# A new table of due times for a planned attention and expert kernel, and two products of zeros ahead of early scores

## The chip, the cores and the metric

One core of one Trainium2 chip runs the whole program. The metric is the device time of one execution in microseconds (us), the median of several runs. The trace comes from one execution taken by the hardware profiler.

## The reference

The inputs are q, k and v of 8 batches, 8 heads, 576 positions and 64 elements, gate weights, and two weight matrices. The first half is attention in a window: each position looks at itself and at the 63 positions ahead of it.

```python
scores = scale * np.matmul(q, k.transpose(0, 1, 3, 2))
mask = (rel >= 0) & (rel < 64)
scores = np.where(mask, scores, -1000000000.0)
attn = softmax(scores)              # max subtracted, + 1e-09 in the sum
x = (attn @ v) as (8, 576, 512)
```

The second half scores each of a batch's 576 rows of x against the gate weights, picks the 128 highest, and adds to these rows alone a gated two-layer product:

```python
top_idx = np.argpartition(-scores[b], 128)[:128]
xe = x[b, top_idx]
out[b, top_idx] = xe + sigmoid(scores[b, top_idx])[:, None] * (np.maximum(xe @ w1, 0) @ w2)
```

w1 is 512 x 1024, w2 is 1024 x 512, all in float32.

## The kernel before

**Attention.** The 8 x 9 blocks of 64 positions are taken two at a time, as 36 pairs m (`attend`). For a pair, SP loads q, k and v. PE computes the scores in 32 products (`go_s`, L533) into PSUM room s0, the only one of its kind. For pairs 0 to 8, DVE adds the mask and takes the maxima (L554), ACT the exponentials (L563), PE transposes (L571) and ACT copies (L579). From pair 9 on (`fold`), ACT and DVE merge the two key blocks that a row sees (L594, `copy_predicated` L599), DVE takes the maximum (L606), and after the transposes DVE and GpSimd part them again (L639, L645). PE multiplies by v into PSUM room av, also the only one (`go_pv`, L714). ACT takes out the sums (L734), DVE inverts them (L738) and scales (L742). Then DVE forms the gate score of the 128 rows, the **gate dot** (`gate_dot`, L517), with two inputs from SBUF, and SP stores the rows.

**Choice and experts.** When a batch's five pairs have their gate scores (pair 4 closes batch 0), `choose` ranks the rows with comparisons on DVE (L843, L854) and counts on PE (L898, L939). GpSimd then gathers the chosen rows from DRAM (L963). `moe` transposes them (L988) and forms the two expert products on PE (L1055 or L1120, and L1167) for the groups of batches (0), (1), (2), (3), (4, 5), (6, 7). Each float32 product is made of three, from a high and a low part of both sides. The weights are loaded in 16 steps of 256 KB, eight of w1 and eight of w2, and GpSimd splits each into its parts: **hi** (L484) and **lo** (L488).

**The order.** Every operation is entered with `add` into a list of 1919, with an engine, a planned duration and a due time. `Order.run` plans the whole program before it is issued: at each step it looks, for each engine, at the operations whose predecessors and rooms are planned, finds the earliest start t0, and takes the one with the smallest due among those that can start within SLACK of t0. An operation with a late due is still taken if nothing else can start. DVE operations marked `port` (gate dots, comparisons) with a due under BEFORE may be taken if they can start within YIELD of t0. The order so found is the order of the instructions on each engine, and there is no other choice on the chip; each engine waits in that order for its semaphores. PLACE shifts the due time of single operations, named by their number in the list: loads are 5 to 116, weight steps from 118 on in threes (load, hi, lo), and attention begins at 166. Number 232 is the scores of pair 2 and 265 the scores of pair 3. The same planner carries constants for what it believes of the chip: LINK (a delay between engines ahead of PE), TURN (a change of PE's tile mode), RATE (bytes per us of the transfers), PHASE, FETCH and FRESH (PE's instruction fetch).

After the scores of pairs 0, 1 and 2 the kernel already issues a product of zeros into another PSUM room (`keep_warm`, L310): 256, 256 and 128 columns.

Of the kernel before, what the change touches and what calls it, by code (L numbers as in the profile page):

```python
# [21 lines left out]
P = 128  # L22
# [5 lines left out]
STEP = 4.61  # L28
EASE = 1.1
BEGIN = 6.8  # L30
LINK = {"PE": 0.3404}
TURN = 0.25
RATE = 350700.0
FLIGHT = 6
FIRST = 10
PLACE = {
# [24 lines left out]
}  # L61
PREV = 0.5
CUR = 0.2
BEFORE = 37.46
YIELD = 1.885
FETCH = 256
PHASE = 193
FRESH = 3.401
KEEP = {0: 2, 1: 2, 2: 1}
WARM = 8  # L70
DIRECT = (0,)
# [19 lines left out]
class Order:  # L91
# [3 lines left out]
    def __init__(self):  # L95
        self.ops = []
        self.room = {}
        self.where = {}
        self.tiles = {}

    def rooms(self, kind, names):
        for n in names:
# [4 lines left out]
    def add(self, *a, **kw):  # L107
        op = Op(*a, **kw)
        op.due += PLACE.get(len(self.ops), 0.0)
        self.ops.append(op)  # L110
        return op

# [14 lines left out]
    def run(self, engines, free):  # L127
        for op in self.ops:
            op.left = len(op.after)
            for a, _ in op.after:  # L130
                a.then.append(op)
        held = {"DVE": (0.0, 0.0), "POOL": (0.0, 0.0)}
        avail = {e: [] for e in engines}
        for op in self.ops:
            if not op.left:
                avail[op.eng].append(op)
        mode = None
        wire = 2.0
        flight = []
        code = WARM * 4  # L140
        marks = {}

        def fetched(op, t):
            end = code + op.code
            k = (end - PHASE) // FETCH
            need = PHASE + FETCH * k
            if need <= code or need - FETCH not in marks:
                return t
            share = (need - code) / op.code
            return max(t, marks[need - FETCH] + FRESH - share * op.pitch)  # L150
        done = 0
        self.log = []
        while done < len(self.ops):
            best = None
            for e in engines:
                cand = []
                for op in avail[e]:
                    t, picks = self.ready(op)
                    if t == float("inf"):
                        continue  # L160
                    t = max(t, free[e])
                    if op.port:
                        a, z = held["POOL" if e == "DVE" else "DVE"]
                        if a <= t < z:
                            t = z
                    if op.code:
                        t = fetched(op, t)
                    if op.size and e == "SP" and len(flight) >= FIRST:
                        t = max(t, flight[-FLIGHT] + 0.1)
                    cand.append((t, op.due, op, picks))  # L170
                if not cand:
                    continue
                t0 = min(c[0] for c in cand)
                same = e == "PE" and mode == 64
                c = min((c for c in cand if c[0] <= t0 + SLACK.get(e, 0.0)
                         or c[2].port and c[2].due < BEFORE and e == "DVE" and c[0] <= t0 + YIELD
                         or same and c[2].mode == mode and c[0] <= t0 + STAY),
                        key=lambda c: (same and c[2].mode != mode, c[1]))
                if best is None or c[0] < best[0]:
                    best = c  # L180
            assert best is not None, [(e, [o.due for o in avail[e]]) for e in engines]
            t, _, op, picks = best
            if op.mode and mode and op.mode != mode:
                t = max(t, free["PE"] + TURN)
            for (key, kind), n in zip([k for k in op.take if k[0] not in self.where], picks):
                self.where[key] = n
                self.room[n] = float("inf")
            op.start = t
            if op.code:
                for need in range(PHASE - FETCH, 1 << 20, FETCH):  # L190
                    if need >= code + op.code:
                        break
                    if need >= code:
                        marks[need] = t + (need - code) / op.code * op.pitch
                code += op.code
            if op.mode:
                mode = op.mode
            if op.port:
                held[op.eng] = (t, t + op.pitch)
            free[op.eng] = t + op.pitch  # L200
            if op.size:
                begin = max(wire, t + op.pitch + 0.25)
                wire = begin + op.size / RATE
                op.end = max(wire, begin + 0.2) + 1.997
                if op.eng == "SP":
                    flight.append(op.end)
            else:
                op.end = t + op.dur
            for key in op.give:
                self.room[self.where[key]] = op.end + 0.1  # L210
            avail[op.eng].remove(op)
            for o in op.then:
                o.left -= 1
                if not o.left:
                    avail[o.eng].append(o)
            self.log.append((t, op))
            op.go()
            done += 1


STAY = 0.2035
SLACK = {"PE": 0.00835, "DVE": 0.02651, "ACT": 0.06129}


@with_exitstack
def tile_attention_moe(ctx: ExitStack, tc, q, k, v, wg, w1, w2, outs, B, H, S, D, C):
    nc = tc.nc
# [10 lines left out]
    order = Order()  # L238
# [47 lines left out]
    def make(key, shape, dtype, space="sb", sub=""):  # L286
        tag = order.where[key] + sub
        serial[0] += 1
        t = (p_ps if space == "ps" else p_sb).tile(
            shape, dtype, tag=tag, name=f"{key[0]}{sub}{'_'.join(map(str, key[1:]))}")  # L290
        order.tiles[key, sub] = t
        return t

    def get(key, sub=""):
        return order.tiles[key, sub]

    warm = const.tile([P, P], F32, name="warm")
# [913 lines left out]
    free = {"PE": 2.0, "ACT": 2.6, "DVE": 2.0, "POOL": 6.2, "SP": 0.8}  # L1211
# [40 lines left out]
```

## Time and profile before

| | |
|---|---|
| median of 3 runs | 248.06 us (247.59 to 249.39) |
| the profiled execution | 246.34 us |
| its span, first to last instruction | 244.6 us |
| mean granted clock of TensorE | 0.979 |
| PE busy | 222.1 us (91%) |
| DVE busy | 188.1 us (77%) |
| ACT busy | 149.3 us (61%) |
| POOL busy | 120.1 us (49%) |
| moved by DMA | 47.22 MB |

PE is TensorE's products (PEld its weight loads), DVE is VectorE, ACT is ScalarE, POOL is GpSimd, SP issues transfers. Busy times are sums over the whole span and hide that the stages differ, so the rows below go by stage. The granted clock is that of TensorE as a share of 2.4 GHz; a stretch with 0.5 runs at 1.2 GHz.

### The profile page before, as it was taken

How to read it: one execution, taken by the hardware profiler on the slowest of the kernel's cores; microseconds unless marked ns; L12 is line 12 of the kernel's file. 1: busy time of each engine (PE TensorE's matmuls, PEld its weight loads, DVE VectorE, ACT ScalarE, POOL GpSimd, SP SyncE). 2: the span in 40 equal slices, each digit the busy share in tenths (PEclk: the TensorE clock that was granted, in tenths of full speed). 3: DMA queues.
4: the chain of work that ended last, by engine and by line, in shares of the span. 5: the costliest groups of instructions: out<-in, count | busy, mean ns of one | idle time of the engine just before them, and what ended most of it. 6: DMA issues, size and time to landing. Idle time of an engine off the chain costs nothing. (4 is left out here: it accounts for less than half of the span.)

```text
span 244.6 us, 10376 instructions
## 1 busy us (share of the span) xinstructions
PE 222.1 (91%) x4298; PEld 186.7 (76%) x4298; DVE 188.1 (77%) x560; ACT 149.3 (61%) x478; POOL 120.1 (49%) x160
## 2 busy tenths in 40 slices
PE   8679695949999999999899999989999999999991
PEld 7567584837877778787678888868878898899891
DVE  0587879797898989999997799999997996352220
ACT  2798865445998798797459977847896231022000
POOL 7885867892042535286048725762752581130031
PEclk9999989797999999999999999999999999999999
DMA  6998999896656698687558657354443221120011
GB/s 212 369 338 280 342 335 337 271 335 217 217 159 223 235 321 291 213 240 265 212 178 295 218 157 225 96 196 146 124 143 89 88 90 43 43 82 6 0 46 43
DMA packets 25167, 47.22 MB, mean 193 GB/s; under 512 B 2976, under 2 KB 4000, under 8 KB 25120
## 3 DMA queue, kind: packets, MB, share of 16 engines
q1 hardware_dynamic: 23680, 42.10, 52.3%
q0 software_dynamic: 1296, 4.20, 5.0%
q8 instruction: 34, 0.56, 0.9%
q10 hardware_dynamic: 144, 0.26, 0.3%
q14 instruction: 13, 0.11, 0.1%
HBM read 35.01 MB, written 11.53 MB: 190 GB/s over the span
## 5 line engine op out<-in xcount | busy, mean ns | idle before, releaser
L616 ACT ACTIVATE p<-p,nm 128x64 f32<-128x64 f32 x216 | 59.2, 341 | 0.4
L645 POOL TENSOR_TENSOR pt<-pt,past 128x512 f32<-128x512 f32 x27 | 35.8, 1328 | 41.7 <-ACT pt L630 35.9
L533 PE MATMUL s<-k,q 64*64 64x128 f32 x1152 | 43.0, 287 | 8.4 <-DVE p L599 3.3
L714 PEld LDWEIGHTS av<-v,pt 64*64 64x64 f32 x2176 | 40.0, 138 | 10.7 <-issue 7.9
L714 PE MATMUL av<-v,pt 64*64 64x65 f32 x2176 | 44.1, 226 | 3.3 <-issue 2.7
L533 PEld LDWEIGHTS s<-k,q 64*64 64x64 f32 x1152 | 34.2, 141 | 16.2 <-issue 5.1
L517 DVE CUSTOM_DVE_ANT_0 jk<-x,wgb 128x512 bf16<-128x512 f32 x36 | 34.0, 945 | 0.2
L563 ACT ACTIVATE p<-p,nm 128x128 f32<-128x128 f32 x72 | 23.7, 394 | 12.5 <-DVE nm L554 12.5
L1167 PE MATMUL yp<-w2l,hh 128*128 128x512 f32 (+1 forms) x72 | 27.4, 381 | 0.0
L1167 PE MATMUL yp<-w2h,hl 128*128 128x512 f32 (+1 forms) x72 | 27.4, 381 | 0.0
L1167 PE MATMUL yp<-w2h,hh 128*128 128x512 f32 (+1 forms) x72 | 27.4, 383 | 0.0
L742 DVE TENSOR_TENSOR x<-av,z 128x512 f32<-128x512 f32 x36 | 24.6, 684 | 1.1
L554 DVE CUSTOM_DVE_ANT_0 p<-s,mask 128x128 f32<-128x128 f32 x72 | 16.2, 285 | 11.2 <-PE s L533 11.1
L599 DVE COPY_PREDICATED p<-live,s 128x512 f32<-128x512 uint8 x27 | 19.7, 731 | 3.1 <-ACT p L594 3.1
L624 PE MATMUL t<-ident,p 128*128 128x128 f32 x108 | 20.8, 282 | 0.0
L594 ACT COPY p<-s 128x512 f32<-128x512 f32 (+1 forms) x27 | 15.8, 585 | 6.7 <-PE s L533 4.3
L1199 POOL DMA_INDIRECT out_dram<-xe,idx x7 | 7.4, 1052 | 25.2 <-DVE xe L1190 22.0
L924 POOL TENSOR_SCALAR sel<-slots,diff 128x128 bf16<-128x128 f32 x20 | 16.3, 822 | 6.5 <-DVE diff L908 3.2
L639 DVE TENSOR_TENSOR pt<-t,own 128x512 f32<-128x512 f32 x27 | 18.2, 675 | 1.7 <-PE t L624 1.6
L630 ACT COPY pt<-t 128x512 f32<-128x512 f32 x27 | 15.7, 583 | 4.9 <-DVE pt L639 3.4
L1120 PE MATMUL hp<-xgh,w1l 128*128 128x256 f32 x64 | 18.1, 284 | 0.0
L606 DVE TENSOR_REDUCE nm<-p 128x8 f32<-128x512 f32 x27 | 17.9, 664 | 0.1
(115 smaller groups left out, 462.3 us busy)
## 6 DMA issues: line engine op xcount, KB each, us to landing
v<-in_v SPq DMA_DIRECT2D x36, 260.0 KB, 3.9
q<-in_q SPq DMA_DIRECT2D x36, 256.0 KB, 3.9
out_dram<-x SPq DMA_DIRECT2D x32, 256.0 KB, 3.8
k<-in_k SPq DMA_DIRECT2D x31, 256.0 KB, 4.6
st<-in_w SPq DMA_DIRECT2D x16, 256.0 KB, 4.8
k<-in_k SPq DMA_DIRECT2D x8, 128.0 KB, 4.7
out_dram<-x SPq DMA_DIRECT2D x8, 128.0 KB, 3.3
k<-in_k ACTq DMA_DIRECT2D x1, 256.0 KB
```

The lines of the kernel that those rows point to most:

```text
L517: nc.vector.tensor_tensor_reduce(out=junk()[:n, :E], in0=xf[:n], in1=wgb[:n], op0=ALU.mult, op1=ALU.add, scale=1.0, scalar=0.0, accum_out=acc)
L533: nc.tensor.matmul(s[c * W:(c + 1) * W, r, j], get(("q", m))[rs, j, c], keys(m, c, j, rs), start=True, stop=True)
L563: nc.scalar.activation(pe[:, j, :, r], pe[:, j, :, r], AF.Exp, bias=st_nm[m][:, r, j:j + 1], scale=-1.0)
L599: nc.vector.copy_predicated(out=get(("p", m)).rearrange("p j r w -> p r j w"), mask=live.unsqueeze(1).unsqueeze(1).to_broadcast([P, 2, NP, ...
L616: nc.scalar.activation(pe[:, j, r], pe[:, j, r], AF.Exp, bias=st_nm[m][:, 1, j, r:r + 1], scale=SCALE)
L624: nc.tensor.transpose(get(("t", m, 0))[:, j, :], get(("p", m))[:, j].rearrange("p r w -> p (r w)"), ident)
L639: nc.vector.tensor_tensor(out=parts(make(("pt", m, 1), [P, NP, P], F32)), in0=parts(get(("t", m, 0))), in1=spread(own), op=ALU.mult)
L645: nc.gpsimd.tensor_tensor(out=pt, in0=pt, in1=spread(past), op=ALU.mult)
L714: nc.tensor.matmul(av[cs, r, j * D1:(j + 1) * D1], pt[a][rs, j, cs], get(("v", g // 2))[rs, g % 2, j], start=a == 0 or o == c, stop=a == 1)
L742: nc.vector.tensor_tensor(out=x.rearrange("p j r d -> p r j d"), in0=avv()[:, :, :, :D], in1=st_z[m][:, 1].unsqueeze(3).to_broadcast([P, 2 ...
L1120: nc.tensor.matmul(get(hk)[:, j], w[:, c, js], get(xk, a)[:, c].rearrange("p u c -> p (u c)"), start=(n == 0), stop=(n == 3 * KC1 - 1))
L1167: nc.tensor.matmul(get(yk)[:C, :e1 - e0], get((a, gi, c // per))[:, c % per, u * C:(u + 1) * C], w[:, c, e0:e1], start=(n == 0), stop=(n = ...
```

## The change

The table PLACE gets 195 entries in place of 168, with three decimals; 78 operations stand in both. The planner's constants LINK, TURN, RATE, BEFORE, YIELD, FRESH, STAY and SLACK get new values. For the scores of pairs 2 and 3 the plan sets aside time for a product of zeros, and when their PSUM tile is made, that product is issued into it: 128 columns for pair 2 and 512 for pair 3. The scores then overwrite it.

```diff
-LINK = {"PE": 0.3404}
-TURN = 0.25
-RATE = 350700.0
+LINK = {"PE": 0.333936}
+TURN = 0.250417
+RATE = 357599.0
+FILLER = 0.2134
+FILLERS = {
+    232: 1, 265: 4
+}
 PLACE = {
...
-    25: 1.1, 26: -13.45, 27: -6.34, 29: 15.08, 32: 3.65, 33: -7.23, 34: -7.37, 35: 3.28,
...
-    147: 45.89, 149: -57.16, 151: -3.68, 152: 1.61, 154: 28.29, 155: 39.09, 158: 6.35,
-    162: 15.19, 164: -2.68, 165: 16.0, 194: 6.27, 234: -47.6, 291: 23.22, 310: 34.99, 326: 37.54,
-    329: 10.68, 333: -19.36, 335: -23.59, 377: 36.2, 382: -18.73, 394: 36.94, 399: 13.71,
...
+    14: -4.393, 15: -2.148, 16: -4.178, 17: -6.616, 18: -7.406, 23: -8.744, 24: -15.837,
+    25: 3.122, 27: -4.312, 29: 11.516, 32: 10.221, 35: 17.652, 36: -2.437, 39: -7.451,
...
+    145: 2.298, 146: -8.242, 147: 72.948, 149: -48.498, 150: -48.599, 151: -2.857, 155: 14.518,
+    158: 62.775, 162: 52.367, 163: -1.14, 164: 7.115, 165: 134.475, 184: 6.859, 191: 7.228,
+    192: 0.374, 209: -3.674, 211: -16.654, 213: -29.709, 263: 16.777, 297: 9.069, 306: -23.978,
+    308: -20.45, 326: 27.295, 327: -36.205, 329: 26.066, 337: 39.436, 364: 9.255, 377: 74.148,
+    394: 789.623, 405: 43.06, 424: -53.619, 429: 8.406, 432: 8.727, 465: 13.537, 471: -3.611,
...
-BEFORE = 37.46
-YIELD = 1.885
+BEFORE = 48.6156
+YIELD = 1.67853
...
-FRESH = 3.401
+FRESH = 2.58373
...
+        op.fill = FILLERS.get(len(self.ops), 0)
...
-            if op.mode and mode and op.mode != mode:
+            if op.fill:
+                b = max([free["PE"]] + [self.room[n] for n in picks])
+                if mode == 64:
+                    b = max(b, free["PE"] + TURN)
+                t = max(t, b + FILLER * op.fill + (TURN if op.mode == 64 else 0.0))
+                code += 4
+            elif op.mode and mode and op.mode != mode:
                 t = max(t, free["PE"] + TURN)
...
-                op.end = max(wire, begin + 0.2) + 1.997
+                op.end = max(wire, begin + 0.2) + 1.96706
...
+            self.now = op
...
-STAY = 0.2035
-SLACK = {"PE": 0.00835, "DVE": 0.02651, "ACT": 0.06129}
+STAY = 0.106418
+SLACK = {"PE": 0.0, "DVE": 0.0276741, "ACT": 0.0548276}
...
+        if space == "ps" and order.now is not None and order.now.fill:
+            busy(t, len(shape), order.now.fill)
         return t
+
+    def busy(t, dims, n):
...
+        nc.tensor.matmul(flat[:, :n * P], warm, warm.unsqueeze(1).to_broadcast([P, n, P]),
+                         start=True, stop=True)
```

Numbers of the table that come up below: 17, 24 and 27 are q of pairs 4, 6 and 7; 23 and 26 are v of pairs 5 and 6; 25 is k of pair 6; 147, 162 and 165 are lo of the weight steps 9, 14 and 15; 155, 158 and 164 are hi of 12, 13 and 15; 263, 329 and 429 are the gate dots of pairs 2, 4 and 7. The gate dot of pair 6 has no entry in either table.

## Rows read from the trace of the kernel before

**Rows 1.** Chain of waits, its last part: start us, length us, what.
```profile
213.74 0.44 PE xt L988 x4
214.18 2.79 PE yp L1167 x12
216.97 11.31 PE hp L1120 x96
228.28 8.41 PE yp L1167 x48
```
**Rows 2.** Windows by stage: busy us of each engine, clock, DMA share, GB/s.
```profile
core 0: us, PE busy (x) PEld busy (x) DVE busy (x) ACT busy (x) POOL busy (x), PEclk, DMA share, GB/s
10.00:26.00 16.00, 13.60 (x388) 11.46 (x386) 11.87 (x77) 13.81 (x43) 11.70 (x23) 1.00 0.97 318
26.00:62.00 36.00, 27.32 (x605) 22.72 (x596) 30.70 (x111) 21.48 (x66) 24.19 (x25) 0.86 0.89 299
62.00:200.00 138.00, 134.29 (x2959) 110.55 (x2957) 127.65 (x311) 104.70 (x354) 68.41 (x65) 1.00 0.60 195
200.00:236.70 36.70, 36.70 (x262) 33.00 (x261) 14.48 (x42) 5.44 (x11) 5.84 (x7) 1.00 0.10 34
```
**Rows 3.** Windows around the three stretches of lower clock, the same columns.
```profile
26.00:29.00 3.00, 1.51 (x38) 1.06 (x28) 2.84 (x16) 2.59 (x9) 1.99 (x4) 1.00 0.98 342
29.00:33.00 4.00, 3.44 (x80) 3.48 (x80) 2.98 (x16) 2.56 (x9) 3.90 (x4) 0.57 1.02 317
38.00:42.00 4.00, 1.46 (x42) 0.97 (x34) 3.73 (x19) 1.98 (x8) 3.30 (x3) 1.00 1.02 346
43.00:47.00 4.00, 3.94 (x98) 3.86 (x99) 2.56 (x21) 1.11 (x4) 3.06 (x3) 0.57 0.88 254
51.00:56.00 5.00, 1.84 (x36) 1.61 (x40) 5.00 (x6) 0.74 (x3) 4.92 (x5) 1.00 1.00 360
56.00:61.00 5.00, 5.00 (x91) 3.85 (x83) 3.75 (x8) 3.47 (x12) 0.38 (x1) 0.66 0.56 199
```
**Rows 4.** Timeline of PE: start us, us, what, in brackets idle time and releaser.
```profile
29.55 1.99 PE L533 MATMUL s<-k,q 64*64 64x128 f32 x32 [1.06 <-DMA k<-in_k]
...
42.02 0.73 PE L571 MATMUL t<-ident,p 128*128 128x128 f32 x4 [1.62 <-ACT p L563]
...
52.15 0.66 PE L988 MATMUL xt<-ident,xe 128*128 128x128 f32 x4 [1.34 <-DMA xe<-out_dram,idx]
...
55.25 1.10 PE L533 MATMUL s<-k,q 64*64 64x128 f32 x32 [2.01 <-DVE p L599]
```
**Rows 5.** Instructions of L517: duration in ns, least, median and greatest.
```profile
L517 DVE CUSTOM_DVE_ANT_0 jk<-x,wgb x36: 632/684/6245, 15.4 to 200.5; 128x512 bf16<-128x512 f32 x36
```
**Rows 6.** Timeline of DVE and POOL, 46 to 56 us.
```profile
46.21 1.18 POOL L963 DMA_INDIRECT xe<-out_dram,idx  x1 [0.29 <-DMA k<-in_k]
...
47.90 1.22 POOL L484 TENSOR_SCALAR w2h<-st 128x512 fp32r<-128x512 f32 x2
48.31 6.25 DVE L517 CUSTOM_DVE_ANT_0 jk<-x,wgb 128x512 bf16<-128x512 f32 x1
...
49.07 4.93 POOL L488 TENSOR_TENSOR w2l<-st,w2h 128x512 fp32r<-128x512 f32 x4
...
53.98 1.05 POOL L484 TENSOR_SCALAR w2h<-st 128x512 fp32r<-128x512 f32 x1
```
**Rows 7.** Timeline of PE, keep-warm products and the scores of pairs 2 and 3.
```profile
9.39 0.70 PE L310 MATMUL kw<-warm 128*128 128x256 f32 x2
...
11.40 1.10 PE L533 MATMUL s<-k,q 64*64 64x128 f32 x32 [0.43 <-PE t L571]
12.44 0.49 PE L310 MATMUL kw<-warm 128*128 128x128 f32 x2
...
15.25 1.10 PE L533 MATMUL s<-k,q 64*64 64x128 f32 x32 [0.22 <-DMA k<-in_k]
```
**Rows 8.** Timeline of POOL, the last gather.
```profile
208.74 0.95 POOL L963 DMA_INDIRECT xe<-out_dram,idx  x1 [3.39 <-DVE idxh L955]
```
**Rows 9.** DMA issues: how many, median us from issue to landing.
```profile
xe<-out_dram,idx POOLq DMA_INDIRECT x8, 4.3
```

More of the change, by code (lines that the diff above doesn't have):

```diff
@@ L99, in __init__ @@
         self.tiles = {}
+        self.now = None
     def rooms(self, kind, names):
@@ L291, in make @@
         order.tiles[key, sub] = t
-        return t
+        if space == "ps" and order.now is not None and order.now.fill:
+            busy(t, len(shape), order.now.fill)
+        return t
+    def busy(t, dims, n):
+        flat = t
+        if dims > 2:
+            names = "abcd"[:dims - 1]
+            flat = t.rearrange(f"p {' '.join(names)} -> p ({' '.join(names)})")
+        nc.tensor.matmul(flat[:, :n * P], warm, warm.unsqueeze(1).to_broadcast([P, n, P]),
+                         start=True, stop=True)
     def get(key, sub=""):
```

44 rows, old and new, of the table PLACE are left out of this document.

## Prediction

> **What bounds the kernel now.** I read the chain of waits first. It ends with PE's expert products back to back, 11.31 and 8.41 us of them, and only the last scatter behind [rows 1]; so a microsecond that PE wins earlier is worth one at the end, as long as PE does not run dry later. The windows by stage tell where PE loses: from 10 to 26 us it is busy 13.60 of 16, from 26 to 62 us 27.32 of 36 at a mean granted clock of 0.86, from 62 to 200 us all but 3.7 us, and after 200 us all the time [rows 2]. Nearly all that a better order can give lies ahead of 62 us, where the transfers are busy 0.97 and 0.89 of the time [rows 2]: loads can change places there, but the sum of them can hardly come earlier.
>
> Three losses stand in that stage.
> - **The halved clock.** Three stretches have a granted clock of 0.57, 0.57 and 0.66, and the 3, 4 and 5 us ahead of them are those with an idle PE (1.51, 1.46 and 1.84 us busy) [rows 3]. Of the two levels, 2.4 and 1.2 GHz, 0.57 over 4 us means 2 x 0.43 x 4 = 3.4 us at the lower one; the third gives 2 x 0.34 x 5 = 3.4 us. PE is busy in nearly all of it, so each costs 1.7 us, together 5.1 us. A score block shows it: 1.99 us at 29.55 against 1.10 at 55.25 [rows 4].
> - **The idle time itself**: 1.49, 2.54 and 3.16 us [rows 3], ended by a k transfer, by ACT (which waited for DVE), by the gathered rows and by DVE [rows 4].
> - **VectorE held off.** The gate dot (L517) has a median of 684 ns, but the one at 48.31 us took 6.25 us [rows 5, 6]. GpSimd ran the weight splits of L484 and L488 from 47.90 to past 55 us without a gap worth the name [rows 6], and the DVE work behind the dot, copy_predicated of pair 9 (L599), released the scores of pair 10 only at 55.25 us [rows 4]. That is 5.56 us of DVE, and most of the 3.16 us of PE.
>
> **The change part by part.**
>
> *Two products of zeros.* They are made where the score tile of pairs 2 and 3 is made, so they wait for its one buffer (s0) and not for q and k; scores queued behind them start later by their length unless they were waiting for data. The keep-warm products of 256 and 128 columns take 0.70 and 0.49 us [rows 7], so 128 columns more cost 0.21 us, and five times 128 (one for pair 2, four for pair 3) 1.05 us. Ahead of these scores PE stood idle 0.43 and 0.22 us [rows 7]; that covers 0.65 us, and 0.4 us is left. The bounds are 0 (all covered by longer waits in the new order) and 1.6 us (each paid from start to end: 0.49 and 0.49 + 3 x 0.21). No half-clock stretch stands at these places before, so on the old order they would win nothing; whether the new one needs them the trace of before cannot show.
>
> *The table.* It adds and removes no instruction, and each transfer stays on its queue with its bytes; the cost is in who waits. SP: q of pairs 4 and 6 and v of pair 5 come forward (due 20.2, 29.5 and 24.9 become 13.6, 13.6 and 16.1), v of pair 6 and most weight loads go back by some places, and k of pair 6, whose transfer ended PE's wait at 29.55 us, stays about where it was in the list (30.6 becomes 32.6, among neighbours moved alike). So I take nothing for that wait; what covers the loads that go back is that their data is used later than 26 us, and if one is late, its scores or its split wait as those at 29.55 us did.
> DVE: the gate dots of pairs 2, 4 and 7 go back (23.4, 43.3 and 46.5 become 40.2, 58.7 and 54.9). With BEFORE raised from 37.46 to 48.62 the dot of pair 6 (due 41.9) now belongs to those for which DVE may wait up to YIELD, in the plan. What is behind a waiting dot on DVE is the masking and maximum of the next pair, and for them wait ACT's exponentials and, through s0, PE's next scores.
> POOL: of the splits that ran after 47.9 us, four go to the very end of its list (lo of steps 9, 14 and 15 and hi of 13: due 109, 100, 185 and 108), with lo of 13 behind its hi. Their sum is as before: four lo of 4.93 us together and a hi of 0.61 [rows 6]. A run of that length is still there to be met by a dot; what the table can do is to have no dot in front of it.
>
> *What I take from this.* Clock: between 0 and 5.1 us can come back. I take two of the three stretches, 3.4 us, because the first two follow idle time of 1.49 and 2.54 us that a small shift closes, while the third hangs on the hold. Hold: between 0 and the 3.16 us that PE lost there; I take 1.5 us, about half, since the other dots, too, show how the same pair of engines ends otherwise (a median of 684 ns) [rows 5]. New waits: a table of 195 moved dues meets a chip that its plan only copies. The bounds are -1.5 us (it also closes the idle time of 26 to 29 us) and +3.2 us (one more such place, 1.49 us idle and 1.7 us of clock); I take +1.5 us, one new wait as long as the shortest seen, without a fall of the clock. Fillers +0.4. The constants LINK, TURN, RATE, FRESH and the slacks change only what the plan believes, and cost nothing by themselves.
>
> The sum is -3.4 - 1.5 + 0.4 + 1.5 = **-3.0 us**. The profiled execution took 246.34 us (244.6 us of span and 1.7 around it) and would come to 243.3; the median of the runs shown is 248.06, 1.7 above it, so I forecast 248.06 - 3.0 = **245.1 us**.
>
> *Does it reach the end?* PE does the later work without pause, so it starts it earlier. The last gather is issued at 208.74 and PE turns to its rows at 213.74 us, with 12 products (2.79 us) of other work still to do behind them [rows 1, 8]. At the median of 4.3 us from issue to landing [rows 9] the rows are there at 213.0, so PE may come 0.7 + 2.8 = 3.5 us early even if attention ends no sooner. A gain of 3.0 us fits; a larger one needs DVE to come earlier as well, which its own 5.56 us allow.
>
> **One rule against the trace.** The 6.25 us stand across five splits in a row, four of them of some 1.23 us [rows 6]: DVE did not get its turn between them. The Trainium skill, SBUF - State Buffer, section "SBUF: two separate sides", says that the port pair of the two engines is an exclusive lock, which goes to whoever starts first, for the whole instruction. Taken by itself that would end a dot's wait with the one split then running; the trace disagrees, with 5.56 us of waiting. By the rule the 1.5 us taken above would not be there.
>
> **The rivals.**
> 1. *The hold stays.* The run of splits is as long as before, so one dot meets it again, pair 10's scores are late, and the third stretch at half clock stays with them; one of the first two goes. 248.06 - 1.7 + 0.4 + 1.5 = 248.3, say **248**. For it: the equal length of the run [rows 6]. Against it: three dots are moved back past it. Chance 0.29.
> 2. *The hold is not the splits' doing.* If a dot waits for one split at most, something else made the 6.25 us, and an order cannot remove it: -3.4 + 0.4 + 1.5 = -1.5, **246.6 us**. It is the rule above as a mechanism; the long row of the dot and the run of splits speak against it [rows 5, 6]. Chance 0.05.
> 3. *Slower: the first gather late.* The dot of pair 4 closes batch 0, and its due goes from 43.3 to 58.7. Behind it stand the ranking, the gather (issued at 46.21 us) and the first expert work, begun at 52.15 us [rows 4, 6]. If it slips by six microseconds, PE has only attention for that long, at the 15% idle of 10 to 26 us [rows 2]: 0.9 us, one more half-clock stretch of 1.7, and the fillers' 1.05 with nothing won: **251.7 us**. It decides if PE takes up the first gathered rows after about 58 us. For it: DVE is 85% busy from 26 to 62 us [rows 2], so a late due does wait. Against it: a free DVE starts even a late dot. Chance 0.16.
>
> **How the numbers follow.** The forecast has 0.50, with a range of its own from 241.9 (all three stretches, 5.1, and the 1.5 of the hold, less 0.4) to 247. For all cases I go from 241.9 up to 249.6 (nothing won, fillers at their upper bound of 1.6), which leaves out most of rival 3 and the forecast's best end. A measurement of this kernel can tell about 1% from no change, 245.6 and 250.5 us. Faster: 0.44 of the forecast and 0.01 of rival 1, 0.45. Slower: 0.15 of rival 3 and 0.01 of rival 1, 0.16. Same: 0.39.
>
> **What would show it.** Right: one stretch of half clock at most between 26 and 62 us; no dot over 2 us there; the score blocks of pairs 2 and 3 moved by under 0.5 us; 24 us or more of PE's work between 26 and 62 us, counted at the full clock (27.32 - 5.1 = 22.2 before), and the last expert products about 3 us earlier. Wrong: another dot of 5 us or more (rival 1), the first gathered rows taken up after 58 us (rival 3), PE idle after 62 us until 200 us for much more than the 3.7 us of now [rows 2], or a stretch at half clock at a new place.

## The result, and the profile after

Over 20 runs each, the kernel before has a median of 248.59 us and the kernel after 247.27. Every ratio here and below takes, of each kernel, only the undisturbed runs, those within 1.5% of its fastest, ten of the 20 of after (the profiled executions of e7_w2late, e9_moreload and e11_after are none of them). So taken it is **0.989 (95% interval 0.9855 to 0.9924)**, 1.1% or 2.7 us; the medians of all runs differ by 1.32 us, 0.5%. Forecast were 3.0 us. The profiled execution took 244.62 us against 246.34, 1.7 less. The line numbers have moved by about 32: scores L565, gate dot L549, splits L516 and L520, the products of zeros L323.

The end of the chain of waits after (start us, length us, what) answers to [rows 1]:

```profile
212.97 0.44 PE xt L1020 x4
213.41 1.86 PE yp L1199 x8
215.27 11.31 PE hp L1152 x96
226.58 8.43 PE yp L1199 x48
```

The last expert products begin 1.70 us earlier and last as long. The windows by stage, as in [rows 2] (busy us of each engine, clock, DMA share, GB/s):

```profile
10.00:26.00 16.00, 14.98 (x409) 12.34 (x408) 12.77 (x79) 14.37 (x45) 11.96 (x22) 1.00 0.96 326
26.00:62.00 36.00, 27.70 (x609) 23.58 (x608) 25.43 (x109) 21.86 (x68) 23.31 (x24) 0.86 0.90 304
62.00:200.00 138.00, 134.32 (x2946) 111.31 (x2938) 127.04 (x313) 104.12 (x348) 69.84 (x66) 1.00 0.60 193
```

PE is busy 1.38 us more in the first window and 0.38 in the second, and after that as before. That is not all progress, since the two products of zeros take 1.48 us of the first:

```profile
11.08 0.46 PE L323 MATMUL s<-warm 128*128 128x128 f32 x2 [0.48 <-DVE nm L586]
15.15 1.02 PE L323 MATMUL s<-warm 128*128 128x512 f32 x2
```

The starts of the score blocks tell more: they come 0.92 us earlier at pair 6 (28.63 for 29.55), 1.16 at pair 13 (66.52 for 67.68), and the last expert products 1.70. So some two thirds of the gain lie ahead of pair 13. The clock of the second window is 0.86, as it was. The three stretches are all there, a little earlier (the same columns, each with the idle time ahead of it; they answer to [rows 3]):

```profile
26.00:28.80 2.80, 0.90 (x10) 0.69 (x13) 2.31 (x12) 2.79 (x9) 2.23 (x3) 0.98 0.86 311
28.80:32.00 3.20, 3.20 (x79) 3.20 (x79) 1.33 (x13) 0.94 (x4) 2.04 (x3) 0.50 0.96 353
38.00:42.30 4.30, 2.34 (x30) 1.63 (x31) 4.11 (x21) 1.31 (x5) 3.11 (x4) 1.00 0.99 341
42.30:45.60 3.30, 3.30 (x93) 3.30 (x96) 2.24 (x17) 1.01 (x3) 1.85 (x2) 0.50 0.95 328
46.00:52.50 6.50, 2.87 (x101) 2.15 (x100) 3.57 (x9) 4.03 (x11) 6.40 (x8) 1.00 0.97 291
52.50:56.00 3.50, 3.50 (x40) 3.10 (x40) 1.29 (x2) 1.04 (x3) 3.50 (x3) 0.51 0.87 318
```

What changed is PE's idle time. Its waits between 10 and 62 us (what waited, releaser: us in total, times, longest), first of before, the five longest:

```profile
PE av L714 <- issue: 2.7, 3, 1.3
PE t L571 <- ACT p L563: 2.5, 2, 1.6
PE s L533 <- DVE p L599: 2.0, 1, 2.0
PE xt L988 <- DMA xe<-out_dram,idx: 1.3, 1, 1.3
PE s L533 <- DMA k<-in_k: 1.3, 2, 1.1
```

and of after:

```profile
PE xt L1020 <- DMA xe<-out_dram,idx: 3.5, 1, 3.5
PE s L565 <- DMA k<-in_k: 1.9, 1, 1.9
PE t L603 <- ACT p L595: 1.8, 2, 1.2
PE r L850 <- DVE scores L549: 0.8, 1, 0.8
PE s L323 <- DVE nm L586: 0.5, 1, 0.5
PE s L565 <- DVE nm L586: 0.5, 1, 0.5
```

Gone are 2.7 us in which PE waited for nothing that the trace shows ("issue", three pauses inside the products by v of early pairs) and the 2.0 us for the scores of pair 10. In their place stand 2.2 us more for the first gathered rows, 0.6 more for k and three waits of 0.5 to 0.8 for DVE. The dot that was held off for 6.25 us, that of pair 6 [rows 6], now passes:

```profile
46.06 1.18 POOL L995 DMA_INDIRECT xe<-out_dram,idx  x1 [0.63 <-PE av L746]
47.28 1.65 POOL L516 TENSOR_SCALAR w2h<-st 128x512 fp32r<-128x512 f32 x2
47.29 1.17 DVE L549 CUSTOM_DVE_ANT_0 jk<-x,wgb 128x512 bf16<-128x512 f32 x1
48.88 0.51 POOL L618 MEMSET p<- 64x512 f32 x1
49.37 2.47 POOL L520 TENSOR_TENSOR w2l<-st,w2h 128x512 fp32r<-128x512 f32 x2
```

The splits still run without a gap from 47.28 us, and the dot meets them with the first. It is done between the two hi (1.65 us for both, where they take 1.22 in [rows 6]); the memset of pair 9 stands behind them, and stood ahead of them before:

```profile
47.40 0.54 POOL L586 MEMSET p<- 64x512 f32 x1
```

The gather is issued hardly earlier than before (46.06 against 46.21) and took 6.4 us to land, the longest of all, where the median of the eight is 3.8; the transfers were busy 0.97 of that time. Its rows are taken up at 52.48 us, against 52.15 [rows 4]: PE waits longer for them in the main because it comes earlier.

### The profile page after: what moved, and what is told of

It is laid out like the page before. It is cut to its first block, busy times and chain, and to the rows that moved or that the text cites. A ratio compares the mean times of both kernels' runs of the same rounds, so it can differ in the third digit from the quotient of the medians.

```text
span 242.9 us, 10392 instructions
## 1 busy us (share of the span) xinstructions
PE 222.3 (92%) x4304; PEld 187.6 (77%) x4304; DVE 181.6 (75%) x560; ACT 149.3 (61%) x478; POOL 120.5 (50%) x160
## 4 chain that ended last, share of the span: by engine, by line
PE 42%; DVE 6%; issue 2%; DMA 1%; POOLq 0%
PE yp L1199 14%; PE hp L1152 9%; PE av L746 6%; PE hp L1087 3%; PE s L565 3%; PE t L656 2%; PE xt L1020 1%; DVE p L631 1%; DMA out_dram<-xe,idxh 1%; PE lo L930 1%; PE r L850 1%; DVE cmp L875 1%; DVE x L774 1%; DVE pt L671 1%; PE ht L1116 1%
## 5 line engine op out<-in xcount | busy, mean ns | idle before, releaser
L677 POOL TENSOR_TENSOR pt<-pt,past 128x512 f32<-128x512 f32 x27 | 36.6, 1355 | 35.9 <-ACT pt L662 35.7
L565 PE MATMUL s<-k,q 64*64 64x128 f32 x1152 | 42.8, 286 | 6.7 <-DVE nm L586 1.9
L565 PEld LDWEIGHTS s<-k,q 64*64 64x64 f32 x1152 | 33.8, 140 | 14.8 <-issue 7.4
L746 PE MATMUL av<-v,pt 64*64 64x65 f32 x2176 | 43.5, 226 | 0.8 <-issue 0.6
L549 DVE CUSTOM_DVE_ANT_0 jk<-x,wgb 128x512 bf16<-128x512 f32 x36 | 29.9, 830 | 0.2
L1231 POOL DMA_INDIRECT out_dram<-xe,idx x7 | 8.1, 1158 | 25.6 <-DVE xe L1222 25.3
L656 PE MATMUL t<-ident,p 128*128 128x128 f32 x108 | 19.8, 282 | 0.0
L956 POOL TENSOR_SCALAR sel<-slots,diff 128x128 bf16<-128x128 f32 x20 | 16.1, 811 | 5.8 <-PE t L656 3.2
```

The source lines that it names most:

```text
L549: nc.vector.tensor_tensor_reduce(out=junk()[:n, :E], in0=xf[:n], in1=wgb[:n], op0=ALU.mult, op1=ALU.add, scale=1.0, scalar=0.0, accum_out=acc)
L565: nc.tensor.matmul(s[c * W:(c + 1) * W, r, j], get(("q", m))[rs, j, c], keys(m, c, j, rs), start=True, stop=True)
L656: nc.tensor.transpose(get(("t", m, 0))[:, j, :], get(("p", m))[:, j].rearrange("p r w -> p (r w)"), ident)
L677: nc.gpsimd.tensor_tensor(out=pt, in0=pt, in1=spread(past), op=ALU.mult)
L746: nc.tensor.matmul(av[cs, r, j * D1:(j + 1) * D1], pt[a][rs, j, cs], get(("v", g // 2))[rs, g % 2, j], start=a == 0 or o == c, stop=a == 1)
```

## The experiments

Theory A at the start: the products of zeros, by keeping PE busy, give back the clock. Theory B: they cover pauses in which PE's instructions are late. Then: is the gathered rows' wait, or the transfers as a whole, what paces the stage up to 62 us (theory T), and what was the hold worth (theory H)? The experiments e1 to e4 ran on one chip, e5 to e8 on a second, e9 to e12 on a third, each beside the kernel before; the record does not name the chip of the result. In e3, e4, e7, e8 and e12 the plan is made as in the kernel after and single operations are moved in the order that it gives: each triple in the diffs is the first operation that moves, how many move, and the operation behind which they go, by their numbers in the list.

### e1_nofill: the new order without its products

```diff
-            busy(t, len(shape), order.now.fill)
+            pass
```

> The changed kernel with its order untouched, the time for the two products of zeros still set aside in the plan, but the products not issued. Theory A, they keep the clock up: without them a stretch at the lower level appears between 10 and 26 us and costs about 1.7 us, less the 1.5 us of the products: time within 0.5 us of the changed kernel, but with a mean clock below 1.00 from 10 to 26 us. Theory B, they only fill a wait in which PE's instructions come in: the pauses in the middle of the early value products, 2.7 us before and nearly none now, come back by 1 to 2.7 us, the clock stays at 1.00, scores of pair 5 start within 0.5 us of 23.25 us, and the time stays within 0.5 us. Theory C, they are a plain cost: scores of pairs 4 to 6 start about 1 us earlier and the time falls by up to 1 us (ratio to the kernel before 0.985 to 0.987).

Ratio to before 1.002 (0.997 to 1.008); median 253.71 against 251.66, both of all runs. PE's pauses are back (start us, length us, what, idle time and releaser):

```profile
19.69 0.40 PE L565 MATMUL s<-k,q 64*64 64x128 f32 x2 [1.25 <-issue]
...
26.41 0.47 PE L746 MATMUL av<-v,pt 64*64 64x65 f32 x17 [0.32 <-issue]
30.45 1.10 PE L565 MATMUL s<-k,q 64*64 64x128 f32 x32 [2.77 <-DMA k<-in_k]
```

The first two rows are such pauses, 1.57 us together; the third is a wait for k. The clock is 1.00 from 10 to 26 us without the products, as it is with them and in [rows 2]. Theory A falls: the clock was never low where they stand. The block at 30.45 us runs at full clock too (1.10 us, where [rows 4] has 1.99): the first of the three stretches is absent in this trace, without the products.

### e2_oldfill: the old order with the products

```diff
+        n = {("s", 2): 1, ("s", 3): 4}.get(key, 0)
+        if n:
+            flat = t.rearrange("p a b c d -> p (a b c d)")
+            nc.tensor.matmul(flat[:, :n * P], warm, warm.unsqueeze(1).to_broadcast([P, n, P]),
+                             start=True, stop=True)
```

> The kernel before in its own order, with the two products of zeros issued into the score tiles of pairs 2 and 3 and nothing else changed. As forecast: no stretch at the lower clock stands near them, so they cost 0.4 us, at most 1.6 (ratio 1.002 to 1.006). Theory B of the run without them: the pauses in the middle of the early value products (1.33, 0.41 and 0.98 us) shrink by about the 1.5 us of the products, the scores of pairs 5 and 6 start when they did before (23.83, 29.55 us), and the ratio is 0.998 to 1.002. If the products alone carry the change, the ratio is 0.99.

Ratio 1.002 (0.9985 to 1.006). The pauses shrink to 0.38 and 0.70 us, from 2.7 together. The dot is held 6.78 us here too, and it began before the first split, while the memset ahead of it ran:

```profile
47.50 0.54 POOL L591 MEMSET p<- 64x512 f32 x1
47.88 6.78 DVE L522 CUSTOM_DVE_ANT_0 jk<-x,wgb 128x512 bf16<-128x512 f32 x1
48.00 1.22 POOL L489 TENSOR_SCALAR w2h<-st 128x512 fp32r<-128x512 f32 x2
```

So the products do part of what B says, and by themselves win no time that can be measured.

### e3_xtlate and e4_k6early: taking the two waits away

In e3_xtlate the transposes of the gathered rows go behind the scores of pair 10 and the first six expert products behind those of pair 11; in e4_k6early k of pair 6 is loaded right behind that of pair 5.

```diff
+MOVES = ((1349, 4, 456), (1353, 1, 471), (1354, 1, 493), (1358, 6, 517))   # e3_xtlate
+MOVES = ((25, 1, 22),)                                                      # e4_k6early
```

> The changed kernel with one move on PE, ACT and DVE: the four transposes of the first gathered rows, the copy and the difference that follow them, and the first six expert products go behind the scores of pairs 10 and 11. Theory, the late gather binds: PE's wait of 3.50 us at 48.98 us goes, the scores of pair 10 start at 51 to 51.5 us instead of 54.35, the stretch at the lower clock behind it goes too, and the time falls by 2 to 4 us against the changed kernel (ratio to the kernel before 0.973 to 0.981). Rival, the chain over ACT and DVE binds just behind the gather: scores of pair 10 at most 1 us earlier, ratio 0.985 to 0.992 as without the move.

> The changed kernel with one load moved on SP: k of pair 6 goes right behind k of pair 5, ahead of six other loads and a store. Theory, the load binds the scores of pair 6: its wait of 1.91 us at 26.72 us goes, these scores start at about 26.8 us instead of 28.63, the first stretch at the lower clock goes or is halved, and the time falls by 1.5 to 3.5 us (ratio to the kernel before 0.975 to 0.983). Rival, the ranking of batch 0 on DVE, or a load that was pushed back, takes the gain away: scores of pair 8 start no earlier than 41.8 us (42.26 now) and the ratio stays at 0.985 to 0.992.

Ratios 1.003 (0.999 to 1.007) and 0.998 (0.994 to 1.0025); the unaltered kernel after did not run on this chip. In neither does PE go on; the next transfer is waited for. First e3_xtlate:

```profile
53.86 1.99 PE L565 MATMUL s<-k,q 64*64 64x128 f32 x32 [3.80 <-DMA q<-in_q]
```

That is q of pair 10, 3.80 us in place of the gathered rows' 3.50. In e4_k6early the scores of pair 6 start at 27.98 us, and those of pair 7 pay for it:

```profile
34.47 1.20 PE L565 MATMUL s<-k,q 64*64 64x128 f32 x32 [3.00 <-DMA k<-in_k]
```

Pair 10 starts at 53.86 us where 51 to 51.5 were expected, and pair 8 of e4_k6early at 43.88, no earlier than the 42.26 of after. This speaks for T: one transfer in front of another only passes the wait on.

### e5_after and e6_before: the two kernels on a second chip

> The changed kernel unaltered, next to the runs below on the same chip. If its gain is the same on each chip, the ratio to the kernel before is 0.985 to 0.992; if the four kernels before this one stood at 1.00 because of the chip, it is 0.996 to 1.003.

> The kernel before unaltered, one look, for its trace on this chip. Theory, the transfers and PE's instruction fetches of the first 62 us bind: where the chip is slower, scores of pairs 5, 6 and 12 start later than 23.83, 29.55 and 62.82 us while single instructions keep their durations. Rival, PE or DVE is slower: their mean durations (684 ns of a gate dot, 286 of a score product) differ by over 1%.

Here the gain is not seen: 248.63 against 249.11, ratio **0.999 (0.994 to 1.0035)**; the one execution of e6_before took 250.32. Against the first trace of before its pair 5 starts earlier (22.28 us for 23.83), pairs 6 and 12 later (30.07 and 63.92 for 29.55 and 62.82), and the dots have the same median of 684 ns; the expectation had all three later. The trace of after on this chip tells what the first stretch is worth (a window, columns as above; in the first trace of after its clock is 0.83):

```profile
26.00:36.00 10.00, 7.34 (x196) 6.46 (x190) 8.78 (x51) 7.09 (x22) 5.19 (x7) 1.00 0.95 318
```

The first stretch at half clock did not come, without any edit. The scores of pair 6 start at 29.45 us, 0.82 later than in the first trace of after, those of pair 7 at 33.25 against 33.66, and those of pair 8 at 42.64 against 42.26. So 1.23 us were won between pairs 6 and 7, and 0.79 of them were given back by pair 8. Between the two, PE waits for ACT:

```profile
38.19 0.44 PE L603 MATMUL t<-ident,p 128*128 128x128 f32 x2 [1.32 <-ACT p L595]
40.54 0.73 PE L603 MATMUL t<-ident,p 128*128 128x128 f32 x4 [1.54 <-ACT p L595]
```

These are 2.86 us, against 1.8 in the table above. That PE waits longer because it comes earlier is not shown: in e11_after the same two waits are 3.06 us, with pair 7 at 34.49. But pair 8 hardly follows pair 7: with pair 7 at 30.96 and 31.67 us (e8_all and e12_all) pair 8 starts at 43.06 and 43.01.

### e7_w2late and e8_all: the last four weight loads later

The loads of steps 12 to 15 go behind v of pair 9, their splits and one older lo behind the memset of pair 9; e8_all adds the moves of e3_xtlate and k of pairs 6 and 7 earlier.

```diff
+MOVES = ((154, 1, 35), (157, 1, 154), (160, 1, 157), (163, 1, 160), (147, 1, 465), (155, 2, 163), (161, 2, 156), (158, 2, 162), (164, 2, 159))   # e7_w2late
+MOVES = (... the same nine, (1349, 4, 456), (1353, 1, 471), (1354, 1, 493), (1358, 6, 517), (25, 1, 22), (28, 1, 25))   # e8_all
```

> The changed kernel with the last four weight loads (steps 12 to 15 of w2, 1 MB) moved on SP from between 32 and 38 us behind v of pair 9, and their splits on GpSimd behind the first memset of a merged pair; nothing else moved. The transfers that stood behind them come up to 2.9 us earlier (1 MB at 0.358 MB a us). Theory, the transfers of 26 to 56 us bind PE: scores of pairs 8 and 10 start 1 to 3 us earlier than in the changed kernel beside it, the wait for the gathered rows shrinks from 3.5 to about 1 us if the gather is slowed by the other transfers, and the time falls by 1 to 3 us. Rival, they only change places: another wait (gathered rows, k of pair 6, ACT behind DVE) ends where it did, the scores of pair 12 start within 0.5 us of those of the changed kernel beside it, and the time stays within 0.5 us.

> The changed kernel with the late weight loads, with the first gathered rows taken up behind the scores of pairs 10 and 11, and with k of pairs 6 and 7 loaded right behind k of pair 5. Theory, each wait alone was replaced by the next transfer, and together they go: waits of 1.9 us (k), 3.5 us (gathered rows) and 3.8 us (q of pair 10, seen once the rows were taken up later) shrink to under 2 us in all, the scores of pair 12 start 3 to 5 us earlier than in the changed kernel beside it, and the time falls by 2 to 4 us. Rival, DVE's chain or PE's fetches bind behind them: under 1 us earlier, time within 0.5 us.

Ratios to before 0.988 (0.977 to 0.999) and 0.988 (0.979 to 0.997), on the chip on which after has 0.999. The first rests on two of six runs, and the median of all six, 249.12 us, is that of before, 249.11; so for e7_w2late no gain is shown. Its scores of pair 8 start later than in e5_after (44.04 us for 42.64), those of pair 10 earlier (52.18 for 54.70). In e8_all the scores of pairs 10 to 12 start at 51.19, 53.76 and 58.62 us, against 54.70, 57.99 and 61.09 in e5_after. Then comes the bill (e8_all):

```profile
66.80 1.23 PE L565 MATMUL s<-k,q 64*64 64x128 f32 x32 [2.91 <-DMA q<-in_q]
```

Pair 13 starts at 66.80 us, in e5_after at 66.40. Four loads of 0.26 MB were put off and had to come all the same before that q. Why the ratio should yet be 1% below that of after (give or take 1%), the trace does not show.

### e9_moreload: more transfers

```diff
+    spare = [const.tile([P, 2, 2, W], F32, name=f"spare{i}") for i in range(2)]
...
             move(make(("q", m), [P, NP, 2, W], F32), q[m])
+            if 4 <= m <= 10:
+                move(spare[m % 2], q[m][:, :2])
```

> The kernel after, with a second load of 128 KB behind the q load of each of pairs 4 to 10, into a buffer that nobody reads: 7 x 0.131 = 0.92 MB more on the same queue before about 47 us; nothing else changes. Theory T (up to the scores of pair 13 the transfers set the pace; the windows from 10 to 62 us move 16.15 MB in 52 us, 0.31 MB per us): each load costs 0.42 us, the scores of pair 13 start 2.5 to 3 us later than in the kernel after measured beside it (66.5 then becomes about 69.3), and the end is 2.5 to 3 us later, a ratio to the kernel after of 1.010 to 1.012. Theory C (TensorE's own work and its half-clock stretches set the pace, the loads lie beside it): the scores of pair 13 move by less than 0.8 us, ratio within 0.3% of the kernel after.

Ratio to before 1.018 (1.014 to 1.023), and to the kernel after beside it 1.0182 / 0.9956 = 1.023, 5.6 us: twice what T had. In its trace, of an execution of 256.21 us where the median is 252.85, pair 13 starts at 74.69 us, and T had 69.3. The experiment did more than it should. q of pairs 4 and 6 are loaded one behind the other and both copies go to the same spare buffer, so that SP waits (waits of SP, 10 to 22 us):

```profile
SPq L296 <- DMA spare<-in_q: 2.9, 1, 2.9
```

These 2.9 us are a pause of the queue, and the 0.92 MB of copies at 0.31 MB per us are 3.0 more: 5.9 by T. But the runs that the ratio takes also have a lower clock, 0.964 (median) against 0.979 in e11_after. That more transfers cost time at the end is shown; how much of it is due to the bytes alone is not.

### e10_hold: the splits in the old order

```diff
-    394: 789.623, 405: 43.06, 424: -53.619, 429: 8.406, 432: 8.727, 465: 13.537, 471: -3.611,
+    394: 789.623, 405: 43.06, 424: -53.619, 429: 8.406, 432: 8.727, 465: 2.23, 471: -3.611,
```

> The kernel after, with the due time of one memset (pair 9's pad) at 2.23 instead of 13.537, so that it comes ahead of the weight splits on GpSimd as it did in the kernel before, and the splits run one behind the other again. Theory H (the hold was worth what the prediction took, 1.5 us): a gate dot of 4 to 6 us comes back near 47 us, the scores of pair 10 start 1.5 us or more later than in the kernel after, and the time is 0.5% longer. Theory T (the gathered rows and the transfers end the waits there anyway): the long dot comes back, or does not, but the scores of pair 13 move by less than 0.5 us and the ratio to the kernel after is within 0.3%.

In the plan POOL's list alone changes, by five instructions, and eight tiles of the expert work change places between two buffers. Timeline of POOL and DVE:

```profile
47.25 0.54 POOL L618 MEMSET p<- 64x512 f32 x1
47.75 1.22 POOL L516 TENSOR_SCALAR w2h<-st 128x512 fp32r<-128x512 f32 x2
48.92 2.49 POOL L520 TENSOR_TENSOR w2l<-st,w2h 128x512 fp32r<-128x512 f32 x2
49.10 7.11 DVE L549 CUSTOM_DVE_ANT_0 jk<-x,wgb 128x512 bf16<-128x512 f32 x1
51.38 0.61 POOL L516 TENSOR_SCALAR w2h<-st 128x512 fp32r<-128x512 f32 x1
51.96 3.70 POOL L520 TENSOR_TENSOR w2l<-st,w2h 128x512 fp32r<-128x512 f32 x3
```

and of PE:

```profile
48.02 1.55 PE L565 MATMUL s<-k,q 64*64 64x128 f32 x31
...
52.69 0.66 PE L1020 MATMUL xt<-ident,xe 128*128 128x128 f32 x4 [1.72 <-DMA xe<-out_dram,idx]
56.91 1.99 PE L565 MATMUL s<-k,q 64*64 64x128 f32 x32 [3.12 <-DVE p L631]
```

The dot is held 7.11 us until the run of splits has ended, and the wait of 3.12 us for pair 10's scores is back, beside that for the gathered rows. Ratio to before **1.017 (1.012 to 1.022)**, to after on the same chip 1.0172 / 0.9956 = 1.022, give or take 0.006: 5.4 us. H is right that the hold costs, T wrong that the gathered rows cover it, and both far too low in the time.

The trace explains less than half of the 5.4 us. Pair 10 starts at 56.91 us, 1.7 to 2.6 later than in the traces of after (55.19 on this chip, 54.35 and 54.70), but this execution was late already at pair 9, ahead of the hold: 48.02 us, against 47.26, 46.22 and 46.56. From pair 9 to pair 10 it takes 8.89 us against 7.93 to 8.14, so 0.8 to 1.0 more, and from pair 9 to pair 13 21.97 against 19.84 to 20.30, 1.7 to 2.1 more. The rest fits the clock: the runs that the ratio takes have a median of 0.965 here and 0.979 in e11_after; 0.014 of 250 us is 3.5 us of work at full speed. That is worked out, not shown by an experiment, and part of the lower clock lies ahead of the hold (0.57 from 40 to 48 us, in e11_after 0.79).

### e11_after and e12_all: after once more, and the better order

> The kernel after, unaltered, as the measure for the others of this call, and as a third sample of its gain. If the gain of the first chip is the change's own, the ratio to before is 0.986 to 0.993; if it depends on the chip, 0.997 to 1.002, as on the second. In the trace: scores of pair 13 at 66.4 to 66.6 us under theory T, and a half-clock stretch present or gone at 28 to 32 us without effect on the scores of pair 8 (42.3 to 42.7).

> The kernel after with the last four weight loads and their splits behind the loads that the pairs up to 12 need, the expert work of batch 0 behind the scores of pair 10, and k of pairs 6 and 7 earlier; measured again with more rounds. Theory T: the scores of pairs 10 to 12 start about 3 us earlier than in the kernel after (4 x 0.26 MB at 0.33 MB per us is 3.2 us), and the scores of pair 13 wait for q and start where the kernel after has them, within 0.5 us, since the bytes up to there are the same: ratio to the kernel after within 0.4%. Theory C: the 3 us are kept to the end, ratio to the kernel after 0.988.

After: 248.21 against 248.31, ratio **0.996 (0.992 to 0.9996)**. In its trace, of an execution of 250.19 us, pair 8 starts at 43.34 and pair 13 at 67.11 us, both later than was expected. e12_all, the kernel of e8_all again: 245.26, ratio to before **0.987 (0.982 to 0.991)**, and to after 0.991, give or take 0.006. T expected no difference to after: a miss; the 0.988 of theory C lies within the uncertainty. The scores of pair 13 start at 64.78 us here, and do not wait for q:

```profile
64.78 1.10 PE L565 MATMUL s<-k,q 64*64 64x128 f32 x32 [0.70 <-DVE p L631]
```

The transfers of this execution were faster: 319 GB/s from 10 to 62 us, in that of e8_all 307. Over 52 us that is 0.62 MB, or 2.0 us at 0.31 MB per us, and pair 13 starts 2.02 us earlier. The first two traces of after lie between, with 311 GB/s and 66.52 and 66.40 us; e11_after has 308 and 67.11. It goes together with T; as a faster PE frees buffers and so starts loads earlier, cause and effect are not told apart by it.

## Why the prediction came out, point by point

The size came out only by the ratio of the result (2.7 us for 3.0); by the medians of all runs the gain is 1.3, and on the two chips of e5_after and e11_after it is 0.1% and 0.4%. The path to it was not the one forecast: the clock term failed and the hold was worth more than taken, so that two errors in opposite directions made the sum. That the number came close is in part luck.

- **"Clock: I take two of the three stretches, 3.4 us."** This failed. In the first trace of after none of the three went. The reason given, that a small shift closes the idle time ahead of the first two (1.49 and 2.54 us), did not hold: 1.90 of the 2.8 us and 1.96 of the 4.3 us ahead of them are idle now, ended by k's transfer and by ACT. And whether the first comes is not fixed by the order: e5_after, the same program, and e1_nofill do without it. Where it was absent it gave 1.23 us by the next scores and 0.44 by those behind, not its 1.7.
- **"Hold: 1.5 us."** Right that the hold could go and that it costs; wrong in the way and in the size. The forecast had no dot in front of the run, and three dots moved back past it. But the held dot is that of pair 6, whose due no table shifts, and it still meets the run at 47.29 us; the dots of pairs 2, 4 and 7, with their later dues, run at 24.84, 36.16 and 58.30 us, before at 25.43, 37.26 and 58.48. What spared the dot is the memset of pair 9, number 465, due 11.3 us later, which the prediction does not name. In the four traces with the memset ahead of the splits the dot took 6.25 to 7.11 us, in six with two hi ahead of the memset 0.82 to 1.46 (in the seventh, e9_moreload, it was done before them). Putting the memset back costs 5.4 us on the chip where the whole change wins 1.1 (0.4% of 248). What is left of the new order then stands 1.7% behind before. Whether the move of that one memset would do as much for the kernel before was not tried.
- **"New waits: +1.5 us."** Right in kind: the first gathered rows, 1.34 us before [rows 4] and 3.50 after, and k, 0.6 more. That is 2.8 us for 1.5. The rows came only 0.33 us later, so most of it is a wait that PE met earlier.
- **"Fillers +0.4."** Open. They take 0.46 and 1.02 us, and with them 2.7 us of pauses went, which I had not counted among the losses at all, though the timeline of before had them. Without them 1.57 us of pauses stand in e1_nofill; with them 1.08 in e2_oldfill, 2.2 in e10_hold and 2.4 in e12_all. What they are worth in time no run tells, since e1_nofill had no kernel after beside it.
- **The end.** Right: after 62 us nothing is lost, and the last gather is issued at 207.04 us, 1.7 earlier than in [rows 8].
- **The signs.** As said: no dot over 2 us before 62 us, and the scores of pair 2 moved by 0.07 us. Not as said: three stretches for one at most, the last expert products 1.70 us earlier for about 3, the scores of pair 3 moved by 0.86, and PE's work between 26 and 62 us at full clock, 27.70 - 5.0 = 22.7 us for 24 or more.
- **Rival 1** (the hold stays) did not come, for the dot passed, but its outcome, no gain, is what the chip of e5_after gave, and nearly that of e11_after. **Rival 3** did not come either: the gathered rows are taken up at 52.48 us.
- **Rival 2 and the rule of the Trainium skill** (SBUF - State Buffer, section "SBUF: two separate sides"). The prediction said that the trace disagrees. In the fourteen traces 90 dots began while a split, a memset or a product of the mask ran on POOL; 75 of them took the rest of that one instruction and 0.55 us more (median), as the exclusive lock that the rule tells of would have it; eleven met a memset alone and lost nothing (0.68 us), and a memset reads nothing from SBUF, which the rule asks of GpSimd's side. The remaining four waited through several instructions that POOL ran without a gap, 6.25 to 7.11 us in all. Of 53 dots that began inside a selection of the ranking (`sel`), 13 began 0.05 to 0.08 us behind its start and passed it in 0.67 to 0.68 us, and it was the selection that then took 1.23 to 1.25 us (median 0.72); 19 waited for it and for the product of the mask behind it as well, 1.80 us beyond the selection. So the traces agree with an exclusive lock for most single instructions, and the price of meeting a run is another: DVE need not get its turn between two. In the trace of after it did, between the two hi at 47.28 us. Nor does it hang on whether the dot or the run starts first: in e2_oldfill and e6_before the held dots began 0.12 and 0.40 us ahead of the first split, inside the memset, and in e11_after and e4_k6early dots that began 0.15 and 0.28 us ahead of it passed. What decides that is not shown.

The three ratios of after, 0.989, 0.999 and 0.996, do not agree within their uncertainty: the interval of the first ends at 0.9924, that of the second begins at 0.9937. By the medians of all runs they are 0.995, 0.998 and 1.000. The new order is thus not shown to win more than some tenths of a per cent on every chip; whether the chip or the choice of runs makes the first larger is open.

## What to carry to other kernels

Where transfers are busy nine tenths of a stage, an order of loads chooses which wait is seen: e3_xtlate and e4_k6early took a wait away and met the next one. So count the bytes that must be in by the stage's end before a wait is counted as a gain; they are not all, since e12_all, with the same bytes, is 0.9% faster than after. A two-input VectorE instruction on SBUF that meets GpSimd's back-to-back splits can wait for many of them (7.1 us for 0.7), even where it began first: keep such runs short, or look in the trace at what stands at their head, for moving one memset there brought the wait back here. What a half-clock stretch costs is read at the next waits, not from its lost work alone: of 1.23 us 0.44 were left one pair later, in the one trace that allows the comparison. And a gain of 1% wants more than one chip before it is called one.

## What the runs showed of the hardware

PE's pauses without a cause that the trace shows come and go between executions of the same instructions, and can be dear. In e10_hold one of 2.09 us stands in the midst of the transposes, and e11_after has the same at the same place; the first two traces of after have none there:

```profile
153.55 0.91 PE L1116 MATMUL ht<-ident,n 128*128 128x128 f32 x3 [2.09 <-issue]
```

and the windows behind it show the clock fall:

```profile
150.00:154.00 4.00, 1.91 (x79) 1.65 (x72) 2.46 (x6) 1.09 (x3) 2.54 (x2) 0.92 0.81 236
154.00:158.00 4.00, 4.00 (x15) 3.19 (x14) 2.63 (x5) 2.28 (x10) 0.00 (x0) 0.65 0.17 60
```

From the scores of pair 28 to those of pair 31 this execution takes 19.9 us, and the first two traces of after 16.1. The pause of 2.09 us and the half clock behind it (0.92 and 0.65 over 4 us each, 1.7 us of work at full speed) account for these 3.8 us, more than the change is worth. The 20 runs of after in the result lay 3% apart (243.64 to 251.20 us).
